# Moving the decay of far keys from a TensorE pass into the matrix added before the row maximum, in a fused attention and two-layer FFN kernel

## Chip, cores, metric

One core of one Trainium2 chip. The metric is the device time in microseconds of one execution; the median of three runs of the kernel before is 938.83 us (938.78 to 939.15).

## What is computed

Attention with a forget gate over 4 batches of 8 heads, 576 positions, head size 64; its output, 2304 tokens of 512, goes through two FFN layers of width 2048. All in float32.

```python
scores = scale * np.matmul(q, k.transpose(0, 1, 3, 2))
cum = np.cumsum(np.log(np.clip(f, 0.0001, 1.0)), axis=-1)
decay = cum[:, :, :, None] - cum[:, :, None, :]
scores = np.where(causal, -1000000000.0, scores + decay)
attn = np.exp(scores - np.max(scores, axis=-1, keepdims=True))
attn = attn / (np.sum(attn, axis=-1, keepdims=True) + 1e-09)
x = np.matmul(attn, v)
h = x @ w_in;   x = (h - np.tanh(h)) @ w_out
h = x @ w_in2;  out = (h / (1 + np.exp(-h))) @ w_out2
```

A row of the softmax doesn't change when a constant is added to all its scores, so only the part of the decay that depends on the key matters.

## The kernel before, in words

The attention stage takes the 32 heads as 16 pairs; the two heads of a pair lie on partitions 0 to 63 and 64 to 127, so two matmuls of 64 rows run side by side. A pair has four units of score tiles (`scores`, line 634): unit 0 holds query blocks 0 and 1 (128 rows each, 128 and 256 keys), units 1 and 2 hold blocks 2 and 3 (384 and 512 keys), unit 3 the last 64 queries of both heads together against 576 keys. That makes nine tiles: 2 of 128 keys, 2 of 256, 2 of 384, 2 of 512 and 1 of 576.

q and k are split into a rounded high part and the rest (`split`, line 579, tiles `kqs` from `kqraw`), and a score tile is the sum of four passes into one PSUM bank: high by high, high by low, low by high, and `de` by `de`. The last pass carries the decay: each head has four rows in `de` (high and low part of -cum for the keys, of cum for the queries, each against a row of 1/scale), filled in `decay_rows` (line 106) for all heads at once on 32 partitions, and brought into place by `place_dec` and `place_dec_last`.

A tile then runs through the engines: VectorE adds the mask, scales, and takes the row's extreme (`least`, line 670), ScalarE takes the exponential and the row's sum (`expo`), VectorE the reciprocals for three tiles at a time (`guard`, `normalise`), POOL scales the rows (line 692), TensorE transposes them (`transposes`), VectorE and ScalarE copy the result out of PSUM (line 749), and TensorE multiplies by v (`values`). Two PSUM buffers hold scores.

The order is written out by hand: a loop over steps, one tile each, in which `later(n, ...)` says at which step a function is called, and each engine executes its instructions in that order. The splits of the next pair are called at steps 0, -1, 1, 2, 3 and 4 of a pair (rounding of k on POOL, rounding of q on VectorE, four pieces of low part on POOL). From the third pair on, VectorE and ScalarE also prepare FFN weights in the odd steps (`wjob`). SP issues all DMAs, in order, apart from a few at the start.

At the start `busy` runs 24 matmuls of 512 columns on a zeroed tile while the first inputs arrive, and 16 more stand as fillers between the first pair's units.

```python
for j, k in enumerate((0, -1, 1, 2, 3, 4)):
    later(n0 + k, split, p, j)
later(n0 + 5, place_last, p)
```

Of the kernel before, what the change touches and what calls it, by code (L numbers as in the profile page):

```python
# [7 lines left out]
F32 = mybir.dt.float32  # L8
# [15 lines left out]
NWARM = 24  # L24
# [17 lines left out]
def forgetting_attention_two_ffn(  # L42
# [24 lines left out]
    def setup_masks(const):  # L67
        mask = const.tile([P, 640], F32, name="mask")
        nc.gpsimd.memset(mask, 0.0)
        nc.gpsimd.affine_select(  # L70
            out=mask[:, 512:640], in_=mask[:, 512:640], pattern=[[-1, P]],
            compare_op=ALU.is_ge, fill=MASKED, base=0, channel_multiplier=1,
        )

        sums = const.tile([P, 5, 3, 2], F32, name="sums")
        nc.gpsimd.memset(sums, 1e-9)
        mask4 = const.tile([P, S], F32, name="mask4")
        nc.gpsimd.memset(mask4, 0.0)
        for j in range(2):
            m = mask4[64 * j:64 * j + 64, S - 64:]  # L80
# [4 lines left out]
        return mask, sums, mask4  # L85
# [13 lines left out]
    QS = slice(S, 2 * S)  # L99

    def decay_consts(rows):
        nc.gpsimd.memset(rows[:, 0::2, QS], 1.0 / SCALE)
        nc.gpsimd.memset(rows[:, 1::2, KQ], 1.0 / SCALE)

    def decay_rows(rows, scratch, ft, split):

        ones, lf, cum = scratch

        def r(j, c):
            return rows[:, j, c].bitcast(F32R)  # L110

        nc.vector.tensor_scalar(ft, ft, 1e-4, 1.0, ALU.max, ALU.min)
        nc.scalar.activation(lf, ft, AF.Ln)
        nc.vector.tensor_tensor_scan(cum, ones, lf, 0.0, ALU.mult, ALU.add)
# [421 lines left out]
    def attention(first):  # L536
        with ExitStack() as actx:
# [23 lines left out]
            des = [kp.tile([P, S + 512], F32R, name=f"de{i}") for i in range(2)]  # L561
            lqs = [kp.tile([P, 3, P], F32R, name=f"lq{i}") for i in range(2)]
# [18 lines left out]
            def split(p, j):  # L581
# [4 lines left out]
                if j < 2:  # L586
# [46 lines left out]
            def operands(p):  # L633
                return kqs[p][:, 0], kqs[p][:, 1], des[p % 2]
# [338 lines left out]
```

## Time and profile before

| | |
|---|---|
| median of three runs | 938.83 us |
| the profiled execution | 939.1 us, span 937.1 us |
| granted TensorE clock, mean | 0.999 |
| TensorE busy | 928.8 us, 99% of the span |
| VectorE | 732.0 us, 78% |
| ScalarE | 439.0 us, 47% |
| POOL | 161.4 us, 17% |
| the chain that ended last | TensorE 87%, VectorE 8%, ScalarE 2% |

The shares are means over the whole kernel. The attention stage is the first 185 us, a fifth of the span; POOL works only there, at nine tenths in most slices. The table of stretches gives each engine's busy time between two times; the timeline gives instructions in order, those of one kind merged, with start, length and count, and in brackets the idle time before and what ended it. Lengths of TensorE's rows overlap, so its work is read from one start to the next.

### The profile page before, as it was taken

The numbers are of one execution on the slowest core, as the hardware profiler recorded it, in microseconds if no ns is written. First come the engines' busy times: TensorE is split into PE (matmuls) and PEld (weight loads), VectorE is DVE, ScalarE is ACT, GpSimd is POOL, SyncE is SP. The second block draws the span as 40 slices with busy tenths as digits, with TensorE's granted clock in tenths as the row PEclk, the third lists the DMA queues.
The fourth block names the chain that finished last, engine by engine and source line by source line (L and its number), as shares of the span: only waits on it lengthen the run. The fifth ranks groups of instructions, "written<-read, shape, count | busy, mean of one in ns | idle before, by whom it ended". The sixth has DMA issues, their size and how long they took to land.

```text
span 937.1 us, 14902 instructions
## 1 busy us (share of the span) xinstructions
PE 928.8 (99%) x5532; PEld 846.5 (90%) x5532; DVE 732.0 (78%) x1326; ACT 439.0 (47%) x790; POOL 161.4 (17%) x242
## 2 busy tenths in 40 slices
PE   9999999999999999999999999999999999999998
PEld 6777777799999999999999999888898988888887
DVE  7798998898887887888888998877776667664444
ACT  6889888666353424242424354545342334232311
POOL 8999999200000000000000000000000000000000
PEclk9999999999999999999999999999999999999999
DMA  5424441667557753775367337564875476336722
GB/s 161 152 96 174 140 162 53 258 241 322 192 203 278 280 202 129 277 279 199 151 258 281 147 135 272 188 253 174 326 263 177 176 271 254 140 126 233 246 91 102
DMA packets 45945, 188.88 MB, mean 202 GB/s; under 512 B 9456, under 2 KB 9712, under 8 KB 45840
## 3 DMA queue, kind: packets, MB, share of 16 engines
q1 hardware_dynamic: 45720, 187.77, 54.5%
q8 instruction: 44, 0.72, 0.3%
q14 instruction: 29, 0.24, 0.1%
q10 hardware_dynamic: 152, 0.15, 0.1%
HBM read 148.44 MB, written 38.34 MB: 199 GB/s over the span
## 4 chain that ended last, share of the span: by engine, by line
PE 87%; DVE 8%; ACT 2%; issue 2%; POOL 0%; ACTq 0%; DVEq 0%; POOLq 0%
PE a L384 37%; PE h L416 31%; PE s L657 5%; PE t L704 5%; PE out_t L760 4%; PE s L649 2%; PE h L430 2%; DVE hs L469 1%; PE out_t L788 1%; DVE xo L281 1%; DVE xt L267 1%; DVE wl L193 1%; ACT t L446 1%; DVE gl L459 1%; DVE t L448 1%
## 5 line engine op out<-in xcount | busy, mean ns | idle before, releaser
L416 PE MATMUL h<-xo,wh 128*128 128x384 f32 x1232 | 314.0, 335 | 0.0
L469 DVE TENSOR_TENSOR hs<-h,hs 128x384 f32<-128x384 f32 x308 | 170.6, 554 | 89.8 <-PE h L416 86.3
L416 PEld LDWEIGHTS h<-xo,wh 128*128 128x128 f32 x1232 | 225.4, 188 | 14.1
L446 ACT ACTIVATE t<-hs 128x768 f32<-128x768 f32 x88 | 74.5, 847 | 310.0 <-DVE hs L469 310.0
L416 PE MATMUL h<-xo,wl 128*128 128x384 f32 x616 | 206.9, 336 | 0.0
L384 PE MATMUL a<-gh,wh 128*128 128x384 f32 x384 | 128.6, 335 | 0.9 <-ACT x L398 0.5
L384 PE MATMUL a<-gh,wl 128*128 128x384 f32 x384 | 128.3, 334 | 0.0
L384 PE MATMUL a<-gl,wh 128*128 128x384 f32 x384 | 128.3, 334 | 0.0
L459 DVE TENSOR_TENSOR gl<-t,gh 128x768 fp32r<-128x768 f32 x96 | 91.5, 953 | 34.1 <-ACT gh L455 33.8
L416 PEld LDWEIGHTS h<-xo,wl 128*128 128x128 f32 x616 | 115.6, 188 | 0.0
L384 PE MATMUL a<-wh,gl 128*128 128x512 f32 x284 | 112.6, 396 | 0.0
L384 PE MATMUL a<-wl,gh 128*128 128x512 f32 x284 | 112.2, 395 | 0.0
L384 PE MATMUL a<-wh,gh 128*128 128x512 f32 x284 | 110.6, 389 | 0.4 <-DVE x L400 0.4
L455 ACT CAST gh<-t 128x768 fp32r<-128x768 f32 x96 | 80.4, 838 | 34.0 <-DVE t L448 27.8
L678 ACT ACTIVATE p<-p,mn 128x128 f32<-128x128 f32 (+3 forms) x128 | 71.4, 560 | 17.5 <-DVE mn L670 14.8
L692 POOL TENSOR_SCALAR p<-p,sm 128x128 f32<-128x128 f32 (+3 forms) x128 | 72.9, 588 | 7.4 <-DVE sm L689 7.0
L384 PEld LDWEIGHTS a<-gh,wh 128*128 128x128 f32 x384 | 72.1, 188 | 1.8 <-DVE x L400 1.0
L384 PEld LDWEIGHTS a<-gl,wh 128*128 128x128 f32 x384 | 72.1, 188 | 0.0
L384 PEld LDWEIGHTS a<-gh,wl 128*128 128x128 f32 x384 | 72.1, 188 | 0.0
L670 DVE CUSTOM_DVE_ANT_0 p<-s,mask 128x128 f32<-128x128 f32 (+3 forms) x128 | 59.5, 478 | 13.6 <-PE s L657 13.6
L400 DVE TENSOR_TENSOR x<-a,x 128x768 f32<-128x768 f32 (+2 forms) x60 | 57.0, 950 | 9.1 <-PE a L384 9.0
L384 PEld LDWEIGHTS a<-wh,gl 128*128 128x128 f32 x284 | 53.2, 187 | 11.4
(103 smaller groups left out, 1335.9 us busy)
## 6 DMA issues: line engine op xcount, KB each, us to landing
xo<-xd SPq DMA_DIRECT2D x126, 768.0 KB
xd<-xo SPq DMA_DIRECT2D x42, 768.0 KB
raw<-w_in SPq DMA_DIRECT2D x32, 512.0 KB
raw<-w_out SPq DMA_DIRECT2D x32, 512.0 KB
kqraw<-kq SPq DMA_DIRECT2D x16, 608.0 KB
vraw<-v SPq DMA_DIRECT2D x16, 320.0 KB
out<-ob SPq DMA_DIRECT2D x6, 512.0 KB
out<-ob SPq DMA_DIRECT2D x5, 256.0 KB
```

What stands on the lines that cost most here:

```text
L384: nc.tensor.matmul(dst, w, m, start=first and r == 0, stop=last and r == 2)
L400: nc.vector.tensor_tensor(total, acc, total, ALU.add)
L416: nc.tensor.matmul(dst, w[:, ks], m[:, k], start=k == 0 and r == 0, stop=k == 1 and r == 2)
L446: nc.scalar.activation(t, hs[h], AF.Silu if l else AF.Tanh)
L455: nc.scalar.copy(gh, hs[h])
L459: nc.vector.tensor_tensor(gl, hs[h], rd(gh), ALU.subtract)
L469: nc.vector.tensor_tensor(to, p, s, ALU.add)
L657: nc.tensor.matmul(s[:, h, c:c + n], a[half(h), q], b[half(h), 0:n], start=r == 0, stop=r == 3,)
L670: nc.vector.tensor_tensor_reduce(out=pt.rearrange("p (g c) -> p g c", g=2) if i == 4 else pt, in0=src, in1=m, op0=ALU.add, op1=ALU.min, sc ...
L678: nc.scalar.activation(pt, pt, AF.Exp, bias=mn, scale=-1.0, accum_out=sums[:, n // 3 % 5, n % 3, 0:1],)
L692: nc.gpsimd.tensor_scalar(pt, pt, sm[:, j:j + 1], 1.0, ALU.mult, ALU.mult)
L704: nc.tensor.transpose(t[:, k], pt[:, c * P:c * P + P], ident)
```

## The change

The decay of a key is taken relative to the first position of the query block. For keys in front of the block the term is a row of numbers, the same for each of the 128 queries: it is computed once for all heads on 32 partitions (`decay_far`, on POOL), stored to DRAM (`dfar`), and for each pair read back repeated over 128 partitions into `bias` (64 for `bias4`), which takes the place of the constant mask in `least`. Only the block on the diagonal keeps a `de` pass, now of two rows per head (`near`, high and low) against rows of 1/scale, 128 columns wide, third of the four passes. In unit 0 one strided pass serves both blocks, and the passes run over both blocks in turn. The query's own term is left out, since it is constant in a row.

`bias` has one buffer: its four parts are loaded again for the next pair by `place_far`, at steps 5, 6, 8 and 9, each behind the last tile that reads it. The causal triangles stay in it.

The rounding of q for the next pair goes from VectorE to POOL; the low part of q, two pieces of 320 columns on POOL before, becomes one of 640 on VectorE, called at step 3. There are 18 warm-up matmuls instead of 24.

```diff
-NWARM = 24
+NWARM = 18
...
+    def triangle(m, n):
+        nc.gpsimd.memset(m, 0.0)
+        for c in range(0, P, n):
             nc.gpsimd.affine_select(
-                out=m, in_=m, pattern=[[-1, 64]], compare_op=ALU.is_ge,
+                out=m[c:c + n], in_=m[c:c + n], pattern=[[-1, n]], compare_op=ALU.is_ge,
                 fill=MASKED, base=0, channel_multiplier=1,
             )
...
-        nc.scalar.mul(r(0, KQ), cum, -1.0)
         split(0, 1)
-        nc.vector.tensor_copy(r(1, QS), cum)
-        nc.vector.tensor_tensor(r(3, QS), cum, rows[:, 1, QS], ALU.subtract)
-        nc.vector.scalar_tensor_tensor(r(2, KQ), cum, -1.0, rows[:, 0, KQ], ALU.mult, ALU.subtract)
+        blocks = cum.rearrange("p (i c) -> p i c", c=P)
+        nc.vector.tensor_tensor(
+            near.rearrange("p (i c) -> p i c", c=P), blocks, blocks[:, :, 0:1].to_broadcast([BH, 5, P]), ALU.subtract,
+        )
+        hi, lo = (rows[:, j].bitcast(F32R) for j in range(2))
+        nc.vector.tensor_scalar(hi, near[:, 0:S], -1.0, None, ALU.mult)
+        nc.vector.scalar_tensor_tensor(lo, near[:, 0:S], -1.0, rows[:, 0], ALU.mult, ALU.subtract)
+
+    def decay_far(far, cum, reaches):
+        for i in reaches:
+            n, c0 = P * i, P * (i * (i - 1) // 2)
+            nc.gpsimd.tensor_scalar(
+                far[:, c0:c0 + n], cum[:, 0:n], cum[:, n:n + 1], -1.0 / SCALE, ALU.subtract, ALU.mult,
+            )
...
-                    elif j == 0:
+                    else:
                         nc.gpsimd.tensor_scalar(hi[:, c], raw[p][:, c], 1.0, 1.0, ALU.mult, ALU.mult)
-                    else:
-                        nc.vector.tensor_reduce(
-                            hi[:, c], raw[p][:, c].rearrange("p (n o) -> p n o", o=1), axis=AX.X, op=ALU.max,
-                        )
                     return
                 c0, c1 = ((0, 288), (288, S), (S, S + 320), (S + 320, RAW))[j - 2]
-                eng = nc.vector if p == 0 and j % 2 == 0 else nc.gpsimd
+                if p and j == 4:
+                    c1 = RAW
+                eng = nc.vector if j == 4 or (p == 0 and j == 2) else nc.gpsimd
...
+            def place_far(p, part):
+                for h in range(2):
+                    r = 2 * p + h
+                    if part == 3:
+                        nc.sync.dma_start(out=bias4[half(h), 0:512], in_=dfar[1][r, 3 * P:].partition_broadcast(64))
+                        continue
+                    frm = dfar[part // 2][r, slice(P, 3 * P) if part == 1 else slice(0, REACH[part])]
+                    nc.sync.dma_start(out=bias[:, h, reach(part + 1)], in_=frm.partition_broadcast(P))
...
-                        for r, (a, b) in enumerate(((th, hi), (th, lo), (tl, hi), (td, de))):
-                            nc.tensor.matmul(s[:, g, 0:S // 2], a, b[:, c], start=r == 0, stop=r == 3)
+                        dst = s[:, g, 0:S // 2]
+                        nc.tensor.matmul(dst, th, hi[:, c], start=True, stop=False)
+                        if g:
+                            nc.tensor.matmul(dst[:, S // 2 - 64:], ld, de[:, S - 64:S], start=False, stop=False)
+                        nc.tensor.matmul(dst, th, lo[:, c], start=False, stop=False)
+                        nc.tensor.matmul(dst, tl, hi[:, c], start=False, stop=True)
...
+                blocks = ((0, 0), (1, P)) if u == 0 else ((u + 1, 0),)
+                for r, (a, b) in enumerate(((hi, hi), (hi, lo), (de, de), (lo, hi))):
+                    if r == 2:
+                        for h in range(2):
+                            if u == 0:
+                                dst = s[:, h].rearrange("p (i c) -> p i c", c=P)[:, 0:3:2]
+                                src = b[half(h), 0:2 * P].rearrange("p (i c) -> p i c", c=P)
+                            else:
+                                dst, src = s[:, h, P * u + P:P * u + 2 * P], b[half(h), P * u + P:P * u + 2 * P]
+                            nc.tensor.matmul(dst, a[half(h), S:S + P], src, start=False, stop=False)
+                        continue
...
-                    sps[p, h, i] = (s[:, h, c:c + n], mask[:, 512 - P * i:640], pt[:, c0:c0 + n])
+                    m = bias[:, h, reach(i).start:diagonal(i).stop] if i else bias[:, h, diagonal(1)]
+                    sps[p, h, i] = (s[:, h, c:c + n], m, pt[:, c0:c0 + n])
...
+            for h in range(2):
+                triangle(bias[:, h, diagonal(1)], P)
+            decay_rows(rows, (ones, lf, cum, near), ft, split)
+            decay_far(far, cum, (1, 2))
+            for i in (2, 3):
+                for h in range(2):
+                    triangle(bias[:, h, diagonal(i)], P)
+            decay_far(far, cum, (3, 4))
+            triangle(bias4[:, S - 64:], 64)
...
             place_dec(0)
+            dfar = [dram.tile([BH, n * P], F32, name=f"dfar{n}") for n in (3, 7)]
+            nc.sync.dma_start(out=dfar[0], in_=far[:, 0:3 * P])
+            nc.sync.dma_start(out=dfar[1], in_=far[:, 3 * P:])
             for j in (2, 4, 3, 5):
                 split(0, j)
+            place_far(0, 0)
+            place_far(0, 1)
+            place_far(0, 2)
+            place_last(0)
+            place_far(0, 3)
...
-                for j, k in enumerate((0, -1, 1, 2, 3, 4)):
+                for part, k in enumerate((5, 6, 8, 9)):
+                    later(n0 + k, place_far, p, part)
+                for j, k in enumerate((0, -1, 1, 2, 3)):
                     later(n0 + k, split, p, j)
```

VectorE in the third pair, before, from the rounding of q behind one pair's tiles to the fourth tile of the next (`sm` are row sums, `mn` row extremes, `ptf` transposed rows; a tile's keys are the last number):

```order
L593 TENSOR_REDUCE kqs_487<-kqraw_358 128x640
L749 COPY ptf_106<-t_2_1_451 128x2x2x128
L670 ISA p_0_457,mn_0_0_502<-s_0_456,mask 128x128
L670 ISA mn_0_0_502 128x1
L670 ISA p_0_457,mn_1_0_508<-s_0_456,mask 128x128
L670 ISA mn_1_0_508 128x1
L685 TENSOR_REDUCE sm_512<-sums 128x3
L670 ISA p_0_457,mn_0_1_514<-s_0_456,mask 128x256
L670 ISA mn_0_1_514 128x1
L689 RECIPROCAL sm_512<-sm_512 128x3
L670 ISA p_0_457,mn_1_1_522<-s_0_456,mask 128x256
L670 ISA mn_1_1_522 128x1
```

After the change, from the first tile of that stretch to the fifth:

```order
L672 ISA p_0_489,mn_0_0_532<-s_0_488,bias 128x128
L672 ISA mn_0_0_532 128x1
L672 ISA p_0_489,mn_1_0_540<-s_0_488,bias 128x128
L672 ISA mn_1_0_540 128x1
L687 TENSOR_REDUCE sm_544<-sums 128x3
L672 ISA p_0_489,mn_0_1_546<-s_0_488,bias 128x256
L672 ISA mn_0_1_546 128x1
L691 RECIPROCAL sm_544<-sm_544 128x3
L672 ISA p_0_489,mn_1_1_554<-s_0_488,bias 128x256
L672 ISA mn_1_1_554 128x1
L596 TENSOR_TENSOR kqs_517<-kqraw_388,kqs_517 128x640
L672 ISA p_1_520,mn_0_2_589<-s_1_519,bias 128x384
```

The rounding of q (the reduce of 640 columns) is gone from its place ahead of the copy out of PSUM; the subtraction of 640 columns stands behind the fourth tile, ahead of the fifth, the first of 384 keys.

POOL at the start, before, from the last fills to the end of pair 0's splits (`kqs_170` is pair 0's):

```order
L69 MEMSET mask 128x640
L70 ISA
L70 AFFINE_SELECT mask<-mask 128x128
L76 MEMSET sums 128x30
L78 MEMSET mask_159 128x576
L81 AFFINE_SELECT mask_159<-mask_159 64x64 x2
L599 TENSOR_TENSOR kqs_170<-kqraw_115,kqs_170 128x288
L599 TENSOR_TENSOR kqs_170<-kqraw_115,kqs_170 128x320
```

The same place after the change, from the third scaling of far keys (`x<-x`) on; `kqs_168` is pair 0's, `kqs_268` pair 1's:

```order
L116 TENSOR_SCALAR x<-x 32x384
L116 TENSOR_SCALAR x<-x 32x512
L68 MEMSET bias_154 128x64
L70 AFFINE_SELECT bias_154<-bias_154 64x64 x2
L596 TENSOR_TENSOR kqs_168<-kqraw_116,kqs_168 128x288
L596 TENSOR_TENSOR kqs_168<-kqraw_116,kqs_168 128x320
L832 MEMSET pt_0_112 128x64
L832 MEMSET pt_1_113 128x64
L77 MEMSET ident 128x128
L78 AFFINE_SELECT ident<-ident 128x128
L590 TENSOR_SCALAR kqs_268<-kqraw_118 128x576
L590 TENSOR_SCALAR kqs_268<-kqraw_118 128x640
```

Ahead of these stand the scalings of 128 and 256 columns and six triangles, so POOL's two subtractions for pair 0 now come behind all far keys and triangles, and the rounding of q for pair 1 (128x640) behind them.

## Rows read from the trace of the kernel before

**Rows 1.** Stretches of one pair each, the seven with POOL above 9.7: one, sum, mean.
```profile
79.14:89.02 9.88, 9.88 (x91) 7.46 (x89) 9.88 (x33) 8.07 (x26) 9.88 (x14) 1.00 0.31 108
sum 69.20, PE 69.20 PEld 52.19 DVE 66.23 ACT 57.66 POOL 68.71; mean PE 9.89 PEld 7.46 DVE 9.46 ACT 8.24 POOL 9.82
```

**Rows 2.** The same view of the six other pairs: sum and mean.
```profile
sum 59.33, PE 59.33 PEld 44.75 DVE 51.09 ACT 51.95 POOL 55.93; mean PE 9.89 PEld 7.46 DVE 8.52 ACT 8.66 POOL 9.32
```

**Rows 3.** Timeline of TensorE in one pair: start us, us, engine, line, operation, tiles.
```profile
71.77 0.96 PE L657 MATMUL s<-kqs 64*128 64x512 f32 x6
72.56 0.40 PE L657 MATMUL s<-de 64*128 64x512 f32 x2
...
74.55 0.29 PE L649 MATMUL s<-de,lq 128*128 128x288 f32 x1
74.68 0.57 PE L649 MATMUL s<-kqs,lq 128*128 128x288 f32 x3
...
76.56 0.28 PE L657 MATMUL s<-de 64*128 64x128 f32 x2
76.68 0.57 PE L657 MATMUL s<-kqs 64*128 64x256 f32 x6
77.08 0.28 PE L657 MATMUL s<-de 64*128 64x256 f32 x2
77.20 0.69 PE L657 MATMUL s<-kqs 64*128 64x384 f32 x6
77.72 0.34 PE L657 MATMUL s<-de 64*128 64x384 f32 x2
```

**Rows 4.** Timeline of VectorE in a heavy pair.
```profile
106.17 0.78 DVE L593 TENSOR_REDUCE kqs<-kqraw 128x640 fp32r<-128x640 f32 x1
...
107.89 0.68 DVE L174 TENSOR_TENSOR wa<-wa,wb 128x512 f32<-128x512 f32 x1
...
109.31 1.23 DVE L174 TENSOR_TENSOR wa<-wa,wb 128x512 f32<-128x512 f32 x1
```

**Rows 5.** Timeline of POOL: a lighter pair (38.56, 42.34) and a heavy one (107.98).
```profile
38.56 0.68 POOL L591 TENSOR_SCALAR kqs<-kqraw 128x576 fp32r<-128x576 f32 x1
...
42.34 2.48 POOL L599 TENSOR_TENSOR kqs<-kqraw,kqs 128x288 fp32r<-128x288 f32 x3
...
107.98 1.12 POOL L591 TENSOR_SCALAR kqs<-kqraw 128x576 fp32r<-128x576 f32 x1
```

**Rows 6.** Timeline of the start; its second line comes from the stretch 1.5:8 of TensorE.
```profile
1.79 8.49 PE L788 MATMUL out_t<-de 128*128 128x512 f32 x24 [1.79 <-POOL de L780]
...
1.79 6.42 PE L788 MATMUL out_t<-de 128*128 128x512 f32 x15 [1.79 <-POOL de L780]
...
4.50 1.35 DVE L114 TENSOR_TENSOR_SCAN x<-x 32x576 f32<-32x576 f32 x1 [0.75 <-ACT x L113]
...
6.59 1.80 POOL L81 TENSOR_SCALAR_AFFINE_SELECT mask<-mask 64x64 f32<-64x64 f32 x2
...
8.21 1.50 DVE L599 TENSOR_TENSOR kqs<-kqraw,kqs 128x288 fp32r<-128x288 f32 x2
...
8.47 1.98 POOL L599 TENSOR_TENSOR kqs<-kqraw,kqs 128x288 fp32r<-128x288 f32 x2
...
10.55 0.20 POOL L89 MEMSET ident<- 128x128 f32 x1
...
10.83 0.29 POOL L90 TENSOR_SCALAR_AFFINE_SELECT ident<-ident 128x128 f32<-128x128 f32 x1
...
11.26 0.72 PE L657 MATMUL s<-kqs 64*128 64x384 f32 x6
...
14.05 0.56 DVE L670 CUSTOM_DVE_ANT_0 p<-s,mask 128x384 f32<-128x384 f32 x1
...
24.11 0.77 PE L704 MATMUL t<-ident,pt 128*128 128x128 f32 x5 [0.93 <-POOL pt L692]
```

**Rows 7.** DMA of the stretch 0 to 185 us: queue, packets, MB, share of 16 engines.
```profile
q1 hardware_dynamic: 12114, 26.92, 42.7%
```

More of the change, by code (lines that the diff above doesn't have):

```diff
@@ L560, in attention @@
             ptfs = [pl.tile([P, 2, NPT], F32, name=f"ptf{i}") for i, pl in ((1, ptps[1]), (0, ptps[0]))][::-1]
-            des = [kp.tile([P, S + 512], F32R, name=f"de{i}") for i in range(2)]
-            lqs = [kp.tile([P, 3, P], F32R, name=f"lq{i}") for i in range(2)]
+            des = [kp.tile([P, S + P], F32R, name=f"de{i}") for i in range(2)]
+            lqs = [kp.tile([P, 2, P], F32R, name=f"lq{i}") for i in range(2)]
+            ld = kp.tile([P, P], F32R, name="ld")
             pt4 = [sp.tile([P, 640], F32, name=f"pt4_{i}", bufs=1) for i in range(2)]
@@ new lines, in scores @@
+                for r, (a, b) in enumerate(((hi, hi), (hi, lo), (de, de), (lo, hi))):
[8 more added lines that the diff above has]
+                        continue
+                    for i, c in blocks:
+                        n = P * (i + 1)
+                        q = slice(S + P * i, S + P * i + P)
@@ L656, in scores @@
                         for h in range(2):
                             nc.tensor.matmul(
-                                s[:, h, c:c + n], a[half(h), q], b[half(h), 0:n], start=r == 0, stop=r == 3,
+                                s[:, h, c:c + n], a[half(h), q], b[half(h), 0:n], start=r == 0 and c == 0, stop=r == 3 and i == u + 1,
                             )
@@ L772, in attention @@
             room = x.rearrange("p k t -> p (k t)")[0:BH]
-            rows = room[:, 0:8 * S].rearrange("p (r w) -> p r w", w=2 * S)
-            ft, *scratch = (room[:, S * j:S * j + S] for j in range(8, 12))
+            rows = room[:, 0:2 * S].rearrange("p (r w) -> p r w", w=S)
+            far = room[:, 2 * S:2 * S + 10 * P]
+            ft, ones, lf, cum, near = (room[:, 2560 + 640 * j:3200 + 640 * j] for j in range(5))
+            ft, ones, lf = (t[:, 0:S] for t in (ft, ones, lf))
             nc.sync.dma_start(out=ft, in_=f)
@@ L778, in attention @@
             load_v(0)
-            nc.vector.memset(scratch[0], 1.0)
+            nc.vector.memset(ones, 1.0)
+            nc.vector.memset(cum[:, S:], 0.0)
             nc.gpsimd.memset(rd(des[1]), 0.0)
             nc.vector.memset(rd(des[0]), 0.0)
-            for t in lqs:
+            for t in lqs + [ld]:
                 nc.gpsimd.memset(rd(t), 0.0)
+            for h in range(2):
+                for t in des:
+                    nc.gpsimd.memset(rd(t[64 * h:64 * h + 2, S:]), 1.0 / SCALE)
+                nc.gpsimd.memset(rd(ld[64 * h:64 * h + 2, half(h)]), 1.0 / SCALE)
             def busy(t, count):
@@ L790, in attention @@
             busy(des[1], NWARM)
-            decay_consts(rows)
-            mask, sums, mask4 = setup_masks(const)
-            decay_rows(rows, scratch, ft, split)
+            bias = kp.tile([P, 2, sum(REACH) + 3 * P], F32, name="bias")
+            bias4 = kp.tile([P, S], F32, name="bias4")
+            sums = const.tile([P, 5, 3, 2], F32, name="sums")
+            nc.gpsimd.memset(sums, 1e-9)
+            for h in range(2):
[3 more added lines that the diff above has]
+            for i in (2, 3):
+                for h in range(2):
+                    triangle(bias[:, h, diagonal(i)], P)
+            decay_far(far, cum, (3, 4))
+            triangle(bias4[:, S - 64:], 64)
             warm = const.tile([P, 1], F32, name="warm")
@@ L916, in attention @@
                     normalise(n - 5)
-                run(n, load_kq, load_v, split, place_last, place_dec, place_dec_last)
+                run(n, load_kq, load_v, split, place_last, place_dec, place_far)
                 for fn, *a in ahead.get(n - N, []):
```

71 lines of the change are left out of this document (18 added, 53 removed).

## The prediction

> **What bounds the kernel now.** I read the attention stage only, because the two FFN layers behind it are untouched. The table of stretches comes first, cut at the period of one head pair: in the thirteen periods between 29.70 and 158.23 us TensorE is busy 9.89 of 9.89 us [rows 1, 2], so it sets the pace. The neighbours are close behind. In seven of the thirteen ("heavy", those with POOL above 9.7) POOL is busy 9.82 us and VectorE 9.46 us on average [rows 1]; in the other six POOL 9.32 and VectorE 8.52 [rows 2]. So a shorter TensorE period pays only as far as these two follow. The timeline of TensorE comes next, for what one decay pass costs [rows 3]: start to start, not the printed durations, because matmuls overlap. Then VectorE and POOL, for what the moved split costs [rows 4, 5], and last the start of the kernel, where TensorE is not the bound: it ends its warm-up at 10.28, and at 24.11 it waits 0.93 us for POOL's normalised rows [rows 6].
>
> **The change part by part.**
>
> *Decay passes.* Before, each pair spends on de: two passes of unit 0 at 0.12 us each (76.56 to 76.68, 77.08 to 77.20); unit 1 one third of 0.52 = 0.17, as the three kqs passes of 384 beside it; unit 2 one third of 0.79 = 0.26, taken as 0.25; unit 3 two at 0.13 = 0.26 [rows 3]. Sum 0.92. After: unit 0 one pass of 256 strided columns, 0.12 (the 256-wide row). Units 1 and 2 one pass of 128: between 0.06 (half of a 256-wide one) and 0.12 (the 128-wide row); 0.10 each, since a 128-wide pass costs what a 256-wide one does and seems bound by its weight load, some of which wide neighbours can hide. Unit 3 one matmul of 64 columns: 0.03 to 0.13, I take 0.08. Sum 0.40 (0.27 to 0.49). Gain 0.52 us per pair (0.43 to 0.65), new TensorE period 9.37. It counts from the end of the start-up, 14.3 pairs: 7.4 us (6.1 to 9.3). Running pass by pass over both blocks of unit 0 instead of block by block keeps the twelve kqs matmuls: nothing.
>
> *The moved split.* POOL loses two subtractions of 320 columns (0.82 each, from 2.48 for three) and gains the rounding of q, 640 columns (0.68 for 576, so 0.76): minus 0.88 us [rows 5]. VectorE loses that rounding, a reduce of 0.78, and gains one subtraction of 640 columns, with both inputs in SBUF, right after the fourth tile. The nearest rows are two sums of 512 columns that also read two SBUF tiles: 0.68 at 107.89 and 1.23 at 109.31, the second in the very place where the new one goes and while POOL works [rows 4]. Scaled by 640/512 the quick one gives 0.85 (+0.07); the slow one, with the same 0.55 of waiting, gives 1.40 (+0.62). I take +0.35. POOL pays as well: its rounding of 576 columns beside the quick sum took 1.12 instead of 0.68 [rows 5], so of POOL's 0.88 some 0.4 is left.
>
> So the new split waits on POOL in two ways: by data (q's rounded half) and by access to SBUF. A rule of the Trainium skill bears on this (SBUF — State Buffer, "Who interferes with whom"): a reduce never contends with GpSimd, a two-input tensor operation does, and whoever starts first holds the port for its whole instruction. The rows agree in part: 1.23 against 0.68, while the reduce takes 0.78 in a busy place. By that rule alone the split would always pay for a whole POOL instruction; that is rival C.
>
> In heavy pairs VectorE then needs 9.46 + 0.35 = 9.81, which is 0.44 more than TensorE's 9.37. Over seven pairs that is 3.1 us, of which I let lighter neighbours win back 0.6, since two score buffers let VectorE lag a little: 2.5 given back (0.5 to 3.6, all that the seven gain). The light six need 8.87 and follow TensorE.
>
> *Start-up.* Removed: two row fills, two masks, VectorE's copy of cum and one ACT pass, six warm-ups. Added on POOL, ahead of its two subtractions for pair 0: six tiny fills, six triangles of 128x128, four scalings of 32 rows, and the rounding of q for pair 1 after them. Those two subtractions ended at 10.45 (8.47 + 1.98) [rows 6]. Up to the arrival of cum (5.85, end of the scan [rows 6]) the new fills and two triangles fit. Behind it: two scalings, four triangles, two more scalings, two 64x64 selects. A select costs 0.29 alone (10.83) and 0.90 in VectorE's way (1.80 for two at 6.59), a fill of 128 columns 0.20 [rows 6]; with an estimated 0.5 per scaling (0.68 for 576 columns [rows 5]) this is 4 x 0.5 + 6 x 0.29 + 0.9 for five fills = 4.6 us at best, 8.3 with selects of 0.90. With the subtractions themselves (1.65 to 1.98) they end at 12.1 to 16.1; I take 13.9, as VectorE is in the way only up to about 9.7 (end of its own subtractions [rows 6]). The wait of TensorE moves to unit 1 of pair 0 (11.26 before), and VectorE, whose new split of pair 1 stands ahead of its fifth tile and waits for POOL's rounding of q, ends its sixth tile at about 17.9 instead of 14.6 [rows 6]. Part of that is hidden by the sixteen filler matmuls between pair 0's units. Followed through POOL's queue (normalise, round, normalise), TensorE's wait at 24.11 comes 2.1 us later; 0.9 if the selects are quick, 3.6 if slow. The six warm-ups bring nothing, since TensorE waits for data anyway: 2.1 us lost. The first far rows go through DRAM and back; they are needed by the third tile, and SP's queue stores both blocks before it reads the first, so they wait for the same POOL work and land beside it.
>
> *DMA.* Each pair adds eight broadcasts: 256 packets each of 512, 1024 and 1536 bytes and 128 of 2048, 896 packets, 1.05 MB. In the attention stage 12114 packets, 26.92 MB, take 42.7% of 16 engines over 185 us [rows 7]: 104 ns each, or 21 KB per us. By bytes the new ones take 3.1 us of 16 engines per pair, by count 5.8, on top of 4.2. I take bytes, 7.3 of 9.4, hidden: each broadcast is issued once its last reader is done and has some six tiles, over 6 us, until the next. With nothing to hide it, it is rival E.
>
> **Sum.** The profiled execution took 939.1 (span 937.1). 939.1 - 7.4 + 2.5 + 2.1 = 936.3. The profiled run lies 0.3 above the median of 938.83, so against that median I say **936.0 us**.
>
> **Rivals**
> - A, the forecast: 936.0, its own range 933.8 to 938.0. Chance 0.48.
> - B, all engines follow: the split runs at 0.85 and the start-up loses 0.9. 939.1 - 7.4 + 0.5 + 0.9 - 0.3 = 932.8. For it: POOL gets room, and its stalls are what stretches VectorE's operations. Against: VectorE's 9.46. Chance 0.18.
> - C, the bound moves to VectorE: the split takes 1.40 each time. Heavy pairs need 9.46 + 0.62 = 10.08, longer than today's 9.89, and give back 7 x 0.71 = 5.0. 939.1 - 7.4 + 5.0 + 2.1 - 0.3 = 938.5. For it: the row of 1.23 in the same place. Against: VectorE's busy time already holds such stalls. Chance 0.16.
> - D, slower: POOL's start queue starves TensorE long enough that its clock falls. The first fifteen warm-ups took 6.42 us, 428 ns for 512 columns, which is the pace of 1.2 GHz; the nine behind them take 230 [rows 6]. With 3.6 us lost in the start and as long a stretch at half pace again (6.42/2 = 3.2): 939.1 - 7.4 + 2.5 + 3.6 + 3.2 - 0.3 = 940.7. It decides once TensorE stands still for much longer than the 0.93 us at 24.11, after which it ran on at full pace. Chance 0.13. The Trainium skill (TensorE: Matmul & The Clock Gate, Part 1) says that an idle array falls back to the lower clock; no fall shows in this trace.
> - E, broadcasts bind: by count the engines need 10.0 us per pair, 0.63 above 9.37, 14.3 times 9.0: 939.1 - 7.4 + 9.0 + 2.1 - 0.3 = 942.5. Chance 0.05.
>
> That the passes do not get cheaper at all is excluded: ten matmuls become seven, each no wider.
>
> **How the numbers follow.** About 0.2%, 1.9 us, is what a measurement of this kernel tells from no change: faster is below 936.9, slower above 940.7. Faster: B 0.18, A 0.33, C 0.01 = 0.52. Same: A 0.14, C 0.13, D 0.03, E 0.01 = 0.31. Slower: A 0.01, C 0.02, D 0.10, E 0.04 = 0.17. The range runs from below B to just under D's price, 932.0 to 940.6; it leaves out E, the worse part of D and the best of B.
>
> **What would show it.** Right: a period of 9.4 in light pairs and 9.6 to 9.9 in heavy ones, the new split at 0.85 to 1.40 with a mean near 1.1, VectorE's wait for unit 2's scores gone, and the first wait for normalised rows near 26. Wrong: a period of 9.4 everywhere (B); VectorE busy throughout with periods over 9.9 (C); a pace of 428 ns after 11 us (D); tiles that wait for a DMA of bias in mid-stage (E).

## The result and the profile after

The changed kernel took 952.93 us (median of 4 runs, 952.31 to 953.81) against 938.82 before: ratio 1.015, 95% interval 1.0138 to 1.0163. It is slower by 14 us where 936.0 was forecast. The profiled execution has a span of 950.9 us, before 937.1.

Two numbers of the profiled execution say where it went. The *first product* is the start of the first matmul of 512 columns that multiplies normalised rows by v (pair 0); the *mean period* is the time from there to the same matmul of pair 14, over 14. Before: 29.53 us and 9.82; after: 38.30 us and 10.15. The start lost 8.8, the periods 14 x 0.33 = 4.6; together 13.4 of the 13.8 us in the span. The rest, the FFN layers above all, kept its time within 0.4 us.

**The start.** Stretches of the changed kernel (us, busy time of PE, PEld, DVE, ACT, POOL; granted clock; DMA share; GB/s):

```profile
10.00:20.00 10.00, 3.83 (x18) 2.66 (x19) 1.59 (x9) 1.77 (x7) 9.30 (x20) 0.65 0.30 64
20.00:30.00 10.00, 9.02 (x56) 6.59 (x55) 5.99 (x26) 5.24 (x18) 6.18 (x11) 0.84 0.85 247
```

The first of them before the change, the same view:

```profile
10.00:20.00 10.00, 10.00 (x80) 7.58 (x80) 6.38 (x27) 5.56 (x18) 7.26 (x16) 1.00 0.57 164
```

TensorE went from busy throughout to 3.83 of 10 us, and the clock it was granted fell from 1.00 to 0.65. POOL is the busy one; its timeline there:

```profile
5.63 3.69 POOL L116 TENSOR_SCALAR x<-x 32x128 f32<-32x128 f32 x2
...
11.55 3.62 POOL L116 TENSOR_SCALAR x<-x 32x384 f32<-32x384 f32 x2
...
16.05 1.61 POOL L596 TENSOR_TENSOR kqs<-kqraw,kqs 128x288 fp32r<-128x288 f32 x2
```

The four scalings of the far rows (L116) took 7.31 us, so pair 0's low halves, ready at 10.45 before [rows 6], came at 17.66. TensorE and VectorE waited for that, and for the broadcasts, which read what the scalings write:

```profile
16.90 0.69 PE L658 MATMUL s<-kqs 64*128 64x384 f32 x2 [6.14 <-POOL kqs L596]
...
18.34 3.78 PE L797 MATMUL out_t<-kqs 128*128 128x512 f32 x8
...
33.21 0.77 PE L706 MATMUL t<-ident,pt 128*128 128x128 f32 x5 [1.27 <-POOL pt L694]
```

```profile
18.65 0.42 DVE L672 CUSTOM_DVE_ANT_0 p<-s,bias 128x256 f32<-128x256 f32 x1 [7.40 <-DMA bias<-dfar]
```

The eight fillers at 18.34 take 3.78 us, 0.47 each, with a granted clock of 0.50 from 14 to 22 us, the lower level of 1.2 GHz; the wait for the normalised rows that stood at 24.11 [rows 6] stands at 33.21.

**The periods.** Five stretches of one pair each, in the columns above. By the order of the pairs in [rows 1, 2] the first and the fourth are light, the others heavy:

```profile
47.78:57.80 10.02, 9.87 (x90) 7.15 (x90) 8.87 (x30) 8.23 (x26) 8.23 (x13) 1.00 1.00 281
57.80:67.70 9.90, 9.80 (x90) 7.24 (x90) 9.90 (x34) 8.06 (x26) 8.28 (x13) 1.00 0.84 228
67.70:78.45 10.75, 9.91 (x90) 7.17 (x90) 10.39 (x38) 7.65 (x24) 9.40 (x15) 1.00 0.71 202
78.45:88.73 10.28, 9.88 (x90) 7.18 (x90) 8.18 (x27) 8.13 (x21) 9.33 (x15) 1.00 0.84 285
88.73:99.91 11.18, 10.31 (x91) 7.22 (x90) 10.71 (x37) 9.24 (x30) 9.03 (x13) 1.00 0.73 210
```

Against [rows 1, 2] the seven heavy pairs grew from 9.89 to 10.54 us on average, at most 11.18, with VectorE busy nearly all of the time in the longest. The six light ones came to 9.93; only two of them (38.30 to 47.78: 9.48, and one of 9.52) show the shorter TensorE period. VectorE in the third stretch:

```profile
68.86 1.28 DVE L596 TENSOR_TENSOR kqs<-kqraw,kqs 128x640 fp32r<-128x640 f32 x1 [0.36 <-POOL kqs L590]
70.06 1.28 DVE L172 TENSOR_TENSOR ws<-wa,wb 128x512 f32<-128x512 f32 x1
71.27 0.54 DVE L672 CUSTOM_DVE_ANT_0 p<-s,bias 128x384 f32<-128x384 f32 x1
```

Grouped by form (count, busy us, mean ns of one, idle us before):

```profile
L596 DVE TENSOR_TENSOR kqs<-kqraw,kqs 128x640 fp32r<-128x640 f32 x12 | 14.3, 1194 | 2.8 <-POOL kqs L590 2.7
```

The new subtraction takes 1.19 us where the reduce it replaces took 0.78 [rows 4], and 2.7/12 = 0.22 of waiting for POOL's rounding comes on top.

A full VectorE is not all of it: in the light pair at 78.45 it is busy for 8.18 of 10.28 us. The waits between 45 and 170 us (what waits, for what: us in total, times, longest), two rows of the change and one of before:

```profile
ACT p L680 <- POOL p L694: 17.9, 9, 2.4
POOL p L694 <- DVE sm L691: 15.2, 11, 2.0
```

```profile
POOL p L692 <- DVE sm L689: 2.5, 5, 0.7
```

The list of before has no wait of ScalarE for POOL's rows. POOL and ScalarE in that light pair:

```profile
78.38 1.36 POOL L590 TENSOR_SCALAR kqs<-kqraw 128x640 fp32r<-128x640 f32 x2
79.83 1.24 POOL L596 TENSOR_TENSOR kqs<-kqraw,kqs 128x288 fp32r<-128x288 f32 x1
81.06 1.52 POOL L694 TENSOR_SCALAR p<-p,sm 128x512 f32<-128x512 f32 x2
```

```profile
81.94 0.62 ACT L680 ACTIVATE p<-p,mn 128x384 f32<-128x384 f32 x1 [2.14 <-POOL p L694]
```

Two roundings and a subtraction, 2.60 us, stand ahead of the rows that ScalarE's exponential waits for. So the moved split delays POOL's rows as well as VectorE.

### The profile page after: what moved, and what is told of

It is laid out like the page before. It is cut to its first block, busy times and chain, and to the rows that moved or that the text cites. A ratio compares the mean times of both kernels' runs of the same rounds, so it can differ in the third digit from the quotient of the medians.

```text
span 950.9 us, 15011 instructions
## 1 busy us (share of the span) xinstructions
PE 928.5 (98%) x5478; PEld 842.7 (89%) x5478; DVE 737.4 (78%) x1327; ACT 436.3 (46%) x789; POOL 157.5 (17%) x246
## 4 chain that ended last, share of the span: by engine, by line
PE 76%; DVE 10%; POOL 6%; issue 3%; DMA 2%; ACT 2%; POOLq 0%; DVEq 0%; ACTq 0%; SPq 0%
PE a L382 38%; PE h L414 31%; POOL p L694 2%; DMA bias<-dfar 2%; PE h L428 2%; PE t L706 1%; DVE p L672 1%; PE out_t L762 1%; DVE hs L467 1%; PE s L658 1%; POOL kqs L590 1%; DVE ptf L751 1%; DVE xt L265 1%; POOL kqs L596 1%; DVE wb L164 1%
## 5 line engine op out<-in xcount | busy, mean ns | idle before, releaser
L672 DVE CUSTOM_DVE_ANT_0 p<-s,bias 128x128 f32<-128x128 f32 (+3 forms) x128 | 59.8, 478 | 18.9 <-DMA bias<-dfar 8.7
```

What stands on the lines that cost most here:

```text
L672: nc.vector.tensor_tensor_reduce(out=pt.rearrange("p (g c) -> p g c", g=2) if i == 4 else pt, in0=src, in1=m, op0=ALU.add, op1=ALU.min, sc ...
```

## The experiments

Seventeen kernels, in the order in which they ran. Columns: median us, and first product and mean period of the profiled execution; the medians of before on the same chips were 938.8 to 939.0. In e7 and e10 the profiled execution was the longest one, 960.58 and 955.82 us, so their last two columns may be high.

| run | us | first product | period |
|---|---|---|---|
| the change | 952.93 | 38.30 | 10.15 |
| e1 scalings on VectorE | 949.19 | 34.11 | 10.12 |
| e2 scalings as multiply-add on POOL | 950.0 (1 run) | 35.58 | 10.13 |
| e3 old split | 957.13 | 40.61 | 10.31 |
| e4 no broadcasts after pair 0 | 952.42 | 39.60 | 10.14 |
| e6 old split, no broadcasts | 943.28 | 36.54 | 9.60 |
| e7 old split, tail copies at step 10 | 956.24 | 43.88 | 10.31 |
| e8 fillers | 954.41 | 39.44 | 10.14 |
| e9 = e1, loads moved | 947.98 | 34.62 | 10.14 |
| e10 = e3, tail copies at step 7 | 953.46 | 39.89 | 10.26 |
| e11 = e10, merged broadcasts | 949.07 | 38.42 | 9.94 |
| e12 shared split, step 7 | 947.00 | 37.97 | 9.75 |
| e13 = e11 + e9 + fillers | 939.89 | 31.47 | 9.75 |
| e14 = e13, shared split | 940.32 | 31.12 | 9.75 |
| e15 = e14 without fillers | 939.99 | 32.08 | 9.75 |
| e16 merged broadcasts only | 952.62 | 38.45 | 10.14 |
| e17 = e15, POOL's split later | 944.59 | 34.55 | 9.97 |
| e18 the same, old split | 944.29 | 30.36 | 10.13 |

My theory after the first look was that the four scalings made the loss in the start, and VectorE's new subtraction the one in the periods; the rivals were the broadcasts' transfers and the clock.

**e1, e2: the scalings.** e1 puts L116 on VectorE; e2 leaves it on POOL and writes the same value as a multiply and an add:

```
-            nc.gpsimd.tensor_scalar(
+            nc.vector.tensor_scalar(                                  # e1
...
-  cum[:, n:n + 1], -1.0 / SCALE, ALU.subtract, ALU.mult,
+  -1.0 / SCALE, at8[:, i:i + 1], ALU.mult, ALU.add,                   # e2, at8 = 8 cum_n
```

> The only change against the changed kernel: the four scalings of far keys run on VectorE instead of POOL, where they took 7.3 us (3.69 and 3.62 for two each, 5.63 to 9.32 and 11.55 to 15.17). VectorE's own scaling of 576 columns took 0.51, so about 1.3 us there. Theory (the start is lost to these four instructions, about 9 of the 14 us): POOL's subtractions of pair 0 end near 10 instead of 17.7, the wait for normalised rows that stood at 33.2 comes at 25 to 27, and the kernel takes 944 to 947. Rival (the start is set by the transfers of the far rows through DRAM and back): the first 256-key tile still waits for bias until 15 or later, and the kernel stays above 949.

> The four scalings stay on POOL, but as a product and a sum (cum times -8 plus a per-row constant) instead of a difference and a product. If the form of the operation is what makes them slow, they take about 0.4 to 0.7 each as POOL's normalisation of 128 to 512 columns does (0.40 to 0.87), and the kernel takes 945 to 948. If any operation of this kind with 32 partitions is as slow on POOL, they stay at 1.4 to 2.3 each and the kernel stays at 952 to 954.

On VectorE the four take 1.31 us together (e1), on POOL as multiply-add 2.84 in place of 7.31 (e2, timeline of POOL):

```profile
7.32 1.31 DVE L116 TENSOR_SCALAR x<-x 32x128 f32<-32x128 f32 x4
```

```profile
5.74 1.50 POOL L117 TENSOR_SCALAR x<-x,at 32x128 f32<-32x128 f32 x2 [0.21 <-DVE at L103]
...
9.99 1.34 POOL L117 TENSOR_SCALAR x<-x,at 32x384 f32<-32x384 f32 x2
```

So the form makes them slow on POOL. Whether it is the operators, their order or the tile that the per-row value comes from, which e2 changes together, is not shown; and e2's single run, 950.0, lies above the expected 945 to 948. The first product moves by 4.2 us in e1. The rest was still missing; e1's VectorE shows the next wait:

```profile
13.04 0.42 DVE L672 CUSTOM_DVE_ANT_0 p<-s,bias 128x256 f32<-128x256 f32 x1 [2.02 <-DMA bias<-dfar]
...
24.79 0.42 DVE L672 CUSTOM_DVE_ANT_0 p<-s,bias 128x256 f32<-128x256 f32 x1 [3.09 <-DMA bias<-dfar]
```

Pair 1's third tile waits 3.09 us for a broadcast that SP issued at 18.93, behind the loads of kq for pair 2 and of v. So the expected size, 944 to 947, was missed by 2 us. The time lies where the rival had it (above 949), though the tile that it named starts at 13.04 and not at 15 or later.

**e3, e4, e6: the split and the broadcasts.** e3 restores the old split (POOL three subtractions, VectorE the rounding); e4 and e6 leave out the broadcasts of pairs 1 to 15, so pair 0's decay stands for all heads:

```
-                for part, k in enumerate((5, 6, 8, 9)):          # e4, e6
-                    later(n0 + k, place_far, p, part)
...
-                for j, k in enumerate((0, -1, 1, 2, 3)):         # e3, e6
+                for j, k in enumerate((0, -1, 1, 2, 3, 4)):
...
```

> Only the split of q goes back to what it was before (rounding by a reduce on VectorE behind the ninth tile, low part in two pieces on POOL); the start stays as changed. Theory (VectorE's subtraction of 640 columns, 1.20 us and a wait of 0.36 for POOL, makes VectorE the bound): the heavy periods of 10.3 to 11.2 fall below 9.9, about 5 us are won, 946 to 949. Rival (the broadcasts on the DMA queue make the periods long): no more than 1 us is won. Second rival (POOL, which gets 0.88 us per pair back, becomes the bound): heavy periods of 9.8 to 10.0, 948 to 950.

> The broadcasts into bias are left out from the second pair on (all pairs use the first pair's far rows, so the output is another one); the split and the start stay as changed. If the broadcasts or their place in SP's queue lengthen the periods, 3 to 6 us are won (946 to 950) and the mean period falls from 10.3 to 9.7 or less. If VectorE is the bound, the periods stay within 0.1 us and the time within 1 us of 952.9.

> q's split as before the change, and the far rows of pair 0 kept for all pairs: the 8 broadcasts that each later pair issues are left out, so the output is another one. Theory (in the run with the old split alone the loss came from SP's queue: the copies of the tail of q wait for POOL's low half, and the broadcasts of the next far rows stand behind them): without broadcasts nothing stands behind them, periods fall to 9.4 to 9.6 us in light and at most 9.9 in heavy pairs, and the time is the start's loss less the passes, 942 to 946 us. Rival (POOL cannot carry three subtractions of 320 columns beside its other work): periods stay above 10.3, 952 us or more.

e3 missed the other way: in place of 5 us won, 4.2 were lost, so my theory did not stand by itself. e4 came as the case of a full VectorE had it, e6 within the time of its theory. The four times make a square. With the new split the broadcasts cost 0.5 us (952.9 against 952.4), within the spread of the runs, with the old one 13.8 (957.1 against 943.3). Without broadcasts the new split costs 9.1: between the profiled executions of e4 and e6, which are 10.8 apart, heavy pairs differ by 0.74 us, light ones by 0.39 (7.5 in all), and the start by 3.1. Two stretches of e6 (a light and a heavy pair), and its rounding by form:

```profile
45.97:55.53 9.56, 9.56 (x91) 7.18 (x90) 8.09 (x32) 8.49 (x27) 9.18 (x15) 1.00 0.52 170
84.23:94.62 10.39, 9.91 (x91) 7.26 (x91) 10.03 (x34) 8.82 (x28) 10.31 (x15) 1.00 0.30 101
```

```profile
L592 DVE TENSOR_REDUCE kqs<-kqraw 128x640 fp32r<-128x640 f32 x11 | 8.6, 784 | 0.0
```

Eleven of e6's fourteen periods are below 9.7: here the passes' gain is seen. Its heavy pairs still take 9.85 on average and up to 10.51, with POOL and VectorE both full (10.31 and 10.03 of 10.39). In e3, SP's queue shows why the gain is not seen (issue start, us, issues; then a row of its waits over the whole execution):

```profile
73.47 0.85 SPq L619 DMA_DIRECT2D bias<-dfar  x2
77.28 1.51 SPq L603 DMA_DIRECT2D lq<-kqs  x2
78.89 1.97 SPq L619 DMA_DIRECT2D bias<-dfar  x4
```

```profile
SPq L603 <- POOL p L696: 24.9, 12, 4.8
```

The copies of q's tail (L603) hold the queue from 74.32 to 77.28, until POOL has the low half; four broadcasts stand behind them, and later tiles wait (1.11 us at 87.90). Before the change the same copies wait longer for POOL, but no broadcast stands behind them. How much the transfers take: q1's packets, MB and share of the 16 engines in 40 to 180 us, first with broadcasts (the change), then without (e4):

```profile
q1 hardware_dynamic: 22162, 31.20, 75.6%
```

```profile
q1 hardware_dynamic: 8314, 15.75, 34.3%
```

41% of 140 us over 13.8 pairs is 4.2 us of 16 engines per pair, or about 4, as three other loads (1.6 MB) fall into the first stretch only.

**e7, e10, e11, e16: SP's queue.** Tail copies at another step, and one broadcast for both heads of a pair in place of two:

```
-                later(n0 + 5, place_last, p)
+                later(n0 + 10, place_last, p)                    # e7; 7 in e10 and e11
...
-                    nc.sync.dma_start(out=bias[:, h, reach(part + 1)], in_=frm.partition_broadcast(P))
+                    nc.sync.dma_start(out=bias[:, :, reach(part + 1)], in_=frm.partition_broadcast(P))   # e11, e16; frm: rows r, r + 1
```

> q's split as before the change, broadcasts kept, and the two copies of q's tail issued five steps later (step 10 after the pair's first, behind all broadcasts, in place of 5). Theory (the queue's order was the loss): near the run without broadcasts, periods of 9.4 to 9.9, 943 to 947 us. Rival (the broadcasts themselves, by their transfers or by SP's time to issue them, about 0.5 us each, bind as soon as VectorE no longer does): periods above 10, 949 us or more.

> The old split with broadcasts, as in the third experiment, and the copies of q's tail issued at step 7 in place of 5 (behind the first four broadcasts, at about the time at which POOL has their data; step 10, tried before, made them late for unit 3 by up to 3.4 us). Theory (order in SP's queue was the loss): periods of 9.4 to 9.9 in most pairs, 945 to 949 us. Rival (the transfers bind: the 16 DMA engines were busy for 0.98 and 0.99 of the time in the periods with weight loads): periods of 10.3 or more stay where the share is near 1, 951 us or more.

> As the run with the tail's copies at step 7, and the six broadcasts of 128 rows per pair issued as three, each for both heads; the bytes stay. If SP's time to issue (0.38 us median each, up to 1.6) is part of the loss: 1 to 3 us less than that run. If only the transfers or only the order count: the same within 1 us.

> The changed kernel with nothing but the six broadcasts per pair merged into three. Theory (VectorE's subtraction sets the heavy periods there; leaving all broadcasts out had changed the time by only 0.5 us): 951.5 to 953.5 us, heavy periods 10.7 to 11.2 as they were. Rival (SP's issuing binds too): 948 to 950 us.

e7 missed: unit 3 now waited for the tail (7.7 us in five waits between 50 and 150). e10 gained 3.7 against e3, less than its theory had, and e11 4.4 more with the same bytes, more than the 1 to 3 expected: order and issuing both counted, and neither alone explains e3. One thing that merging removed shows in the waits from 40 to 175 us: in e10 VectorE's rounding of q waits 5.9 us, in five waits, for the load of kq, in e11 not at all. In e16 merging brings nothing, as its theory had it: in the change itself the split sets the periods, not SP. The pair from 47.78, with a DMA share of 1.00, takes 10.02 us in the change and 9.46 in e4, but 9.43 in e1 and 9.43 in e16, which keep the broadcasts, so that loss is not a fixed price of the transfers.

**e8, e9: what else is in the start.** e8 adds 24 matmuls on ready data behind unit 0. e9 is e1 with a third kqraw buffer, pair 2's load third in the queue and v for pair 1 behind the broadcasts:

```
             scores(0, 0)
+            busy(kqs[0][:, 0], 24)                               # e8
...
-            load_kq(2)
-            load_v(1)                                            # e9
...
```

> The changed kernel with 24 filler matmuls of 512 columns behind unit 0 of pair 0, where TensorE waited 6.14 us for the low half of the keys. Theory (a part of the start's loss is TensorE's clock, which fell to 0.65 in 10 to 20 us and 0.84 in 20 to 30): the granted clock stays near 1, the first wait for normalised rows moves from 33.2 to 31 to 32 us, 950 to 951.5 us. Rival (all of the loss is waiting for data, the clock costs nothing): clock near 1, but first wait at 33 and 952.5 to 953.5 us.

> Far rows scaled on VectorE as in the first experiment, and the loads of kq for pair 2 (now third in the queue, with a third buffer) and of v for pair 1 (now after pair 1's broadcasts) no longer ahead of pair 1's broadcasts. Theory (of the 4.6 us that were left of the start's loss there, about 3 were pair 1's third tile, which waited 3.09 for its broadcast behind those loads): that wait falls below 0.5 us, the first product with values starts near 31 instead of 34.1, 945.5 to 947 us. Rival (the broadcast is late because it is issued late or takes its 4 to 6 us in any case): the wait stays at 2 to 3 us, 948.5 to 950 us.

In e8 the clock stays at 1.00 up to 30 us and TensorE is ready earlier (first transposes at 26.41, after the change 28.15), then gives it all back in one wait, the late broadcast of pair 1:

```profile
10.00:20.00 10.00, 9.36 (x48) 6.73 (x45) 1.74 (x9) 1.95 (x8) 9.37 (x19) 1.00 0.29 65
```

```profile
31.09 0.93 PE L658 MATMUL s<-kqs 64*128 64x512 f32 x4 [3.81 <-DVE mn L672]
```

Behind that wait the clock falls after all, to 0.50 from 32 to 34 us. At 954.41 us e8 lies above both what its theory and what its rival had.

In e9 that late broadcast is gone (the wait at pair 1's third tile is zero), but the first product is no earlier: the clock is at half, and POOL's rows are late.

```profile
14.00:16.00 2.00, 2.00 (x6) 1.44 (x5) 1.99 (x6) 0.70 (x4) 2.00 (x3) 0.50 0.98 224
```

Both expectations on the size were misses; each run took one obstacle away and met the next.

**e12 to e15: all together.** The shared split lets POOL round q and subtract its first 320 columns and VectorE the last 320; e13 to e15 combine it or the old one with e9's start and e11's broadcasts:

```
-                eng = nc.vector if j == 4 or (p == 0 and j == 2) else nc.gpsimd
+                eng = nc.vector if (j == 5 if p else j % 2 == 0) else nc.gpsimd   # e12, e14, e15
...
-NWARM = 18
+NWARM = 24                                                       # e13, e14
...
+            busy(kqs[0][:, 0], 8)                                # e13, e14, behind unit 0
```

> Start as changed, copies of q's tail at step 7, and a split between the two: POOL rounds q (0.76) and subtracts its first 320 columns, VectorE subtracts the last 320, so VectorE has half of the new split's 1.22 us and POOL about what it had before the change. Theory (in the changed kernel VectorE's 640-column subtraction stretches the heavy pairs by about 0.6 us each against the run with the old split and no broadcasts): heavy periods of 10.7 to 11.2 fall by 0.3 to 0.6, 945 to 949 us. Rival (POOL is late for VectorE's half, which then waits for the rounding, or the transfers bind): 951 us or more.

> Everything that should help together: scalings on VectorE, loads of kq for pair 2 and v for pair 1 out of the way, 24 warm-ups and 8 fillers behind unit 0 (in the run with early loads the granted clock was 0.50 from 12 to 18 us), old split, tail copies at step 7, merged broadcasts. Theory: first product with values at 31 to 32.5 us (34.6 without the fillers), then the steady state of the merged run: 6 to 9 us less than it, 937 to 942 us. Rival (the start is bound by data at POOL and by the broadcasts, not by the clock): first product at 34 or later, 942 us or more.

> The start of the last run (scalings on VectorE, loads out of the way, 24 warm-ups, 8 fillers), merged broadcasts, tail copies at step 7, and the shared split. Theory (start and steady state add): first product with values at 31 to 32 us as in that run, light periods 9.45 and heavy ones at most 10.3, 933 to 937 us, faster than the kernel before the change. Rival (what the shared split saves on VectorE is lost again once the broadcasts are merged, because both remove the same wait): 939 to 941 us.

> The same kernel with 18 warm-ups and without the 8 fillers behind unit 0, so the data come at the same times and only what TensorE does while it waits differs. Theory (the clock by itself): the granted clock falls to 0.50 for some 6 us from about 12 us, as in the run with early loads, and the first product with values comes 2 to 3 us later: 935.5 to 940 us, 2 to 3 above the run with fillers. Rival (the clock hides behind the wait for data): within 0.7 us of it.

e12 wins 6.5 us over e10, as expected. This heavy pair of e12 takes 10.31 us; VectorE is busy for 8.98 of them, POOL for 10.23, so POOL is full now:

```profile
66.78:77.09 10.31, 9.66 (x91) 7.18 (x90) 8.98 (x34) 8.08 (x24) 10.23 (x16) 1.00 0.77 227
```

e13 brings the first product to 31.47, 6.9 us earlier than e11; place and time are as expected. e14 fell short of its theory and came where its rival had it: mean period as in e13. Taking the fillers out (e15) changed nothing in the median, but it was not the test that it was meant to be. The clock that was to fall at 12 us, as in e9, stayed at 1.00 without fillers:

```profile
14.00:16.00 2.00, 1.83 (x12) 1.32 (x12) 1.50 (x5) 1.68 (x6) 2.00 (x3) 1.00 0.94 252
```

So e15's first product, 32.08 against e9's 34.62, came without fillers, from the shared split, the merged broadcasts and the later tail copies, which these runs do not separate in the start. The clock fell later, where TensorE waits once more for POOL:

```profile
25.41 0.76 PE L706 MATMUL t<-ident,pt 128*128 128x128 f32 x5 [1.92 <-POOL pt L694]
...
27.09 1.91 PE L706 MATMUL t<-ident,p 128*128 128x128 f32 x8
```

Eight transposes take 1.91 there and 1.04 in e14. In e14's eleven runs clock and time go together: six with a mean clock of 0.999 or 1.0 took 939.9 to 940.3, five with 0.998 took 941.5 to 942.0. In e13, where the lowest is 0.999, the times go up to 942.47, so the clock is not the only thing that varies.

**e17, e18: POOL's order.** Last idea: POOL does its roundings ahead of a pair's last normalise, and TensorE waits for that in heavy pairs. Moved behind it, with the tail copies at step 9 (e17) and 8 (e18):

```
-                for j, k in enumerate((0, -1, 1, 2, 3, 4)):
+                for j, k in enumerate((3, 2, 3, 3, 4, 7)):       # e17; e18: (3, -1, 3, 3, 4, 4)
```

> The version with the new start and the shared split, without the 8 fillers (its best runs were the lowest, 938.9), and POOL's roundings and subtractions for the next pair moved behind the normalise of step 2 (steps 2, 3, 3, 3, 4; VectorE's half at step 7, tail copies at step 9). Theory (POOL's rounding of 1.5 to 1.8 us ahead of the last normalise makes TensorE wait for those rows in heavy pairs, 4.2 us in six waits): the waits go, heavy periods at most 9.9, 934 to 937 us. Rival (POOL is full in heavy pairs, 9.9 of 9.95 us, so another normalise is late instead): 938.5 to 941 us.

> The same new start and merged broadcasts with the old split, its work on POOL also behind that normalise (steps 3, 3, 3, 4, 4; VectorE's rounding of q where it was), tail copies at step 8. Theory: POOL's part of the loss goes as above, but VectorE is busy throughout the heavy pairs here: 936 to 939 us. Rival: nothing gained against the same without the shift (939.9): 939 to 941 us.

Both got slower, by more than their rivals had, and both expectations failed. In e17 those waits went, but the tail's copy was late in pair 1 and unit 0's scores later on (VectorE waited 16.9 us for TensorE in 13 waits). In e18 VectorE waited 8.8 us, in six waits, for POOL's rounding of k. The row is e17's:

```profile
27.08 0.58 PE L636 MATMUL s<-kqs,lq 128*128 128x288 f32 x1 [2.58 <-DMA lq<-kqs]
```

No version beat the kernel before. e13's and e15's ratios are 1.0012 (to 1.0022 and 1.0021).

## Why the prediction was wrong

Two steps failed. The start was to lose 2.1 us and lost 8.8; the periods were to gain 7.4 - 2.5 = 4.9 and lost 4.6. Of these 16.2 us the larger part, 9.5, lies in the periods: some 5 in the moved split, the rest in pairs where the cheaper passes could not count.

*Decay passes: right in kind, at the low end of the range.* 0.52 us per pair was given, 0.43 to 0.65. The periods where TensorE alone is the bound are 9.43 to 9.48, so 0.41 to 0.46. It counted in few pairs, not in 14.3: even with the old split and no broadcasts (e6) the periods gain 14 x (9.82 - 9.60) = 3.0 us in place of 7.4, since the heavy ones, with POOL and VectorE full, keep 9.85.

*The start: the first failed step, 2.1 us given, 0.9 to 3.6, measured 8.8.* The term mis-sized is the "estimated 0.5 per scaling (0.68 for 576 columns [rows 5])": 7.31 us in place of 2.0. The row I took it from multiplies twice, the scaling subtracts a value per row first; the multiply-add form took 2.84. The selects ran at 0.29, which the working has as its best case, 12.1 for the end of the subtractions; with 5.3 more for the scalings that is 17.4, measured 17.66. But taking the scalings out (e1) returned only 4.2 of the 8.8 us; two more points were missing. The far rows do "land beside" POOL's work, 1.0 us behind it (18.65), but the third tile's scores were ready by 10.75: it waited 7.40 us for them alone, and 2.02 even with the scalings out of POOL's way. And pair 1's broadcasts were counted as hidden, while the bulk loads stood ahead of them (3.09). POOL's late data was then followed by rival D's mechanism, which stood at 0.13: the clock granted fell to 0.65 and 0.84 in two stretches of 10 us. The Trainium skill (TensorE: Matmul & The Clock Gate, Part 1) says an idle array falls back to the lower clock; this trace agrees: the array idled 6.14 us and ran on at 0.47 us per 512 columns.

*The moved split: the second failed step, 2.5 us given back, measured about 7.5 (e4 against e6).* VectorE's operation came to the top of its range: 0.35 was taken, and it costs 1.19 - 0.78 = 0.41 more and waits 0.22, in all 0.63, which is rival C's price of 0.62. What failed is the step from there to the period. C priced the heavy pairs at 10.08, and they came to 10.54; the "light six need 8.87 and follow TensorE", at 9.37, and they came to 9.93. The text saw that POOL pays as well, but not who waits for POOL then. Its subtraction beside VectorE's takes 1.24 us (0.80 at 83.27), with the rounding of q ahead of it; POOL's rows come late, ScalarE waits 17.9 us for them, and POOL 15.2 us for VectorE's reciprocals. How much of the longer periods each of these waits makes is not shown; that the split makes them is, by e4 against e6.

The rule of the Trainium skill (SBUF — State Buffer, "Who interferes with whom") agrees with these rows: the reduce took 0.78 to 0.82 in every run that has it, while thirteen of the fifteen subtractions of 640 columns took 1.16 to 1.42. In the other two (0.82) POOL paid in their place; two normalisings that take 1.52 at 81.06 took 2.72 beside one of them:

```profile
90.00 0.82 DVE L596 TENSOR_TENSOR kqs<-kqraw,kqs 128x640 fp32r<-128x640 f32 x1
```

```profile
89.94 2.72 POOL L694 TENSOR_SCALAR p<-p,sm 128x512 f32<-128x512 f32 x2
```

*DMA hidden: right for this split only.* The broadcasts take about 4 us of 16 engines per pair, between the 3.1 by bytes that I took and the 5.8 by count. From pair 1 on they cost 0.5 us at most. That the old split would have lost 13.8 us to them, by SP's order, I had not looked for: the prediction counted transfers and never SP's time to issue, 0.38 us for each of the broadcasts.

By the chances: C came nearest to the cause in the periods (0.16), D in the start (0.13). Their signs appeared, periods over 9.9 with VectorE full and a pace near 428 ns after 11 us; E's did not, as no tile waited for a DMA of bias behind 38 us. The text priced each alone, so nothing above 942.5 was in view. But both together, at its own prices, make 939.1 - 7.4 + 5.0 + 3.6 + 3.2 - 0.3 = 943.2, still 9.7 short.

**What stays open.** With all repairs the mean period is 9.75, not 9.45. POOL (10.23 of 10.31) or VectorE is full in heavy pairs, depending on the split; the attempt on POOL's order failed. How much of e3's loss is transfer time and how much issuing was not separated further. Why e8 is slower than the change, and what in e15 spares the fillers, stays open too.

## What to carry to other kernels

A price for an operation should come from a row of the same form (operators, operand kinds, engine), not of the same size: here the four scalings took 7 us instead of 2. When a small data path is rerouted through DMA, list what stands ahead of and behind each issue in its queue; a copy that waits for another engine delays every issue behind it. Waits in a start stand behind each other, so removing one shows the next: e1 won 3.7 us, e9's loads 1.2 more, e8's fillers lost 1.5; put together in e13 such repairs won 9.2 over e11, with the first product 6.9 us earlier. And an operation moved between two engines delays those that wait for either, so its price is more than its own length.

## What was not expected of the hardware

On POOL, two scalings with 384 columns in all took 3.69 us and two with 896 took 3.62, so the size hardly matters; the multiply-add form takes 1.50 and 1.34. On VectorE all four take 1.31. Merging two broadcasts into one, with 31 to 32 MB either way in 40 to 180 us, saved 4.4 us (e11 against e10): the median issue takes 0.40 us for both heads in place of 0.38 for one, so SP issues the same bytes in half the time. In the change itself that brought nothing (e16).
